# One core, attention times a gated MLP in float32: work queued by the time of its input, sums shared by load, x through two queues, and the first chunk normalised and transposed tile by tile

## The chip, the cores and the metric

The kernel runs on one core of a Trainium2 chip. The number that counts is the device time of one execution in microseconds. Three timed runs of the kernel before lie between 2642.64 and 2644.13 us, with a median of 2642.66 us.

A core has five engines with a queue each: TensorE (PE, matmuls), VectorE (DVE), ScalarE (ACT), GpSimd (POOL) and SyncE (SP), which here does nothing but issue transfers. Each works through its queue in the order in which the program was written; an instruction whose input is missing holds up all that stand behind it on that engine.

## What is computed

With x of 2048 tokens by 576 features, 32 heads of 18 features, and an inner width of 4608:

```python
xn = _layernorm(x, axis=-1)
s = _A_ref(xn, A_wqkv, A_wo)             # softmax attention with 32 heads, then @ wo
g = _silu(_B_ref(xn, B_w_gate, B_w_up, B_w_down))   # ((xn @ w_gate) * (xn @ w_up)) @ w_down
return x + s * g
```

All of it is in float32. Most products are made of two parts: a value is split in a rounded one (the "high" part, written by ACT as float32r) and what is left (the "low" part, a subtraction on DVE or POOL), and the matmul adds high by high, high by low and low by high.

## The kernel before

The program has three stages.

**Opening.** x comes in four chunks of 512 tokens, each of four tiles of 128. `norm_stats` (L287 to L289) and `norm_apply` (L297 to L300) normalise a tile on DVE, with one square root on ACT; `to_columns` (L319 to L327) turns a chunk into columns: PE transposes into PSUM banks, ACT writes the high part, DVE the low one. `qk_block` (L336 to L346) makes 128 of the 1152 columns of q and k for a chunk with 14 matmuls, in the order of the list `PAIRS`; ACT and DVE split the result into one of three `hl` buffers, and SP stores it in DRAM (`sqk`). `w_fetch` loads two blocks of weights, `w_now` splits them (L119 on ACT, L121 on POOL). `v_fetch` loads half of v's weights into a single buffer, which `v_split` (L384, L385) has to have read before the next load. All of this stands in the order of the code.

**Main stage.** `order` writes it with a planner. The array is used as two halves of 64 rows, half 0 and half 1, each with a clock of its own in the plan (`clk`). For each of the 32 heads there are 64 score blocks whose row maxima DVE takes (L541, L543), and 64 blocks made again the other way round, on which ACT takes the exponential (L580, L582); `pv_group` (L591) multiplies them with v on the whole array, three groups a head. Between these the planner spreads the MLP: 72 units, four chunks of tokens (`c`) by 18 steps (`q`). In a unit half 0 makes two "up" blocks and half 1 two "gate" blocks (L629, 27 matmuls each); ACT copies up (`us`, L636), DVE multiplies it with gate (L643), ACT writes the high part `hs` (L646) and POOL the low part (L653). Then both halves make the down products (L677), eight sums a unit. A sum is added to the accumulator by DVE (L734), or copied out by ACT (`st`, L728, two buffers) and added by POOL (L697): the first half of the columns always on DVE, the second always through ACT and POOL (`by_act`).

The planner holds for each engine the time at which it comes free (`free`) and writes an instruction at once when the matmul that it belongs to is written: L646 right after L643, on whose result it waits. Only POOL's work is kept in a list until its input counts as done (`pool_later`). Transfers are written when the planner reaches them, whether or not what they read is made.

**Change of chunk.** While the last gate and up blocks of a chunk run, the tile `xg` that they read is overwritten with the next chunk: after every third matmul one block of x for that half (`x_block`, L356 and L359), ten transfers for each half, all on SP. This happens three times.

**Ending.** The attention's output is multiplied with wo tile by tile (L1249) and joined with g and x.

## Time and profile before

| | us |
|---|---|
| median of the timed runs | 2642.66 |
| the profiled execution: its own time | 2645.09 |
| the profiled execution: span from first to last instruction | 2643.3 |
| PE, DVE, ACT, POOL busy | 2608.3, 1803.8, 1545.8, 663.2 |
| opening: first matmul of `qk_block`, first score block | 16.86, 204.4 |
| main stage, to the first transpose of the ending | 2568.7 |

A page of the profile gives busy time by engine, the chain of work that ended last and the costliest groups of instructions; the trace behind it answers with timelines, with tables of who waited for whom, and with busy time by stretch. PE is busy nearly all the time; a matmul's end is modelled, so PE can count as busy while its next matmul is late.

### The profile page before, as it was taken

How to read it: one execution, taken by the hardware profiler on the slowest of the kernel's cores; microseconds unless marked ns; L12 is line 12 of the kernel's file. 1: busy time of each engine (PE TensorE's matmuls, PEld its weight loads, DVE VectorE, ACT ScalarE, POOL GpSimd, SP SyncE). 2: the span in 40 equal slices, each digit the busy share in tenths (PEclk: the TensorE clock that was granted, in tenths of full speed). 3: DMA queues.
4: the chain of work that ended last, by engine and by line, in shares of the span. 5: the costliest groups of instructions: out<-in, count | busy, mean ns of one | idle time of the engine just before them, and what ended most of it. 6: DMA issues, size and time to landing. Idle time of an engine off the chain costs nothing.

```text
span 2643.3 us, 59231 instructions
## 1 busy us (share of the span) xinstructions
PE 2608.3 (99%) x24504; PEld 2131.3 (81%) x24504; DVE 1803.8 (68%) x3007; ACT 1545.8 (58%) x3096; POOL 663.2 (25%) x683
## 2 busy tenths in 40 slices
PE   7999999999999999999999999999999999999999
PEld 6899888777778887777778877878878778878779
DVE  7218677777777777766667777777767777766336
ACT  4223666666766666656656665666656666656642
POOL 3114543433422112212111211111111212111125
PEclk9999999999999999999999999999999999999999
DMA  6799766676664444464464444444464444533356
GB/s 216 224 302 261 213 192 181 186 189 176 176 172 131 136 145 146 153 168 147 137 171 125 156 142 136 140 127 152 138 161 127 145 135 152 146 123 127 118 195 205
DMA packets 201581, 434.30 MB, mean 164 GB/s; under 512 B 81216, under 2 KB 130784, under 8 KB 167776
## 3 DMA queue, kind: packets, MB, share of 16 engines
q1 hardware_dynamic: 199072, 422.26, 53.8%
q0 software_dynamic: 2240, 8.26, 0.8%
q8 instruction: 192, 3.15, 0.5%
q14 instruction: 77, 0.63, 0.1%
HBM read 314.64 MB, written 110.56 MB: 161 GB/s over the span
## 4 chain that ended last, share of the span: by engine, by line
PE 94%; DMA 2%; DVE 2%; ACT 2%; POOL 0%; issue 0%; SPq 0%; POOLq 0%; ACTq 0%
PE pg L629 34%; PE pg L591 17%; PE pg L677 15%; PE pa L541 10%; PE pb L580 9%; PE pg L1249 2%; PE pg L393 2%; PE pa L336 2%; PE pb L336 2%; ACT pt L582 1%; DMA wor<-in_A_wo_dram 0%; DVE xn L298 0%; DMA xc<-sx 0%; DMA ks<-sqk 0%; DMA swo<-wor 0%; DVE st L287 0%
## 5 line engine op out<-in xcount | busy, mean ns | idle before, releaser
L543 DVE TENSOR_REDUCE mx<-pa 128x1 f32<-128x512 f32 x2016 | 1347.0, 686 | 308.8 <-PE pa L541 175.0
L629 PE MATMUL pg<-xc,wgu 64*128 64x512 f32 x7776 | 1414.2, 393 | 3.7 <-DMA xc<-sx 2.2
L582 ACT ACTIVATE pt<-pb 128x512 f32<-128x512 f32 x2003 | 1135.3, 600 | 462.8 <-PE pb L580 340.9
L629 PEld LDWEIGHTS pg<-xc,wgu 64*128 64x128 f32 x7776 | 1064.2, 186 | 61.4 <-DMA xc<-sx 3.1
L677 PE MATMUL pg<-wd,hs 64*128 64x288 f32 x6816 | 840.2, 293 | 0.0
L677 PEld LDWEIGHTS pg<-wd,hs 64*128 64x128 f32 x6816 | 782.5, 185 | 13.3 <-issue 2.5
L541 PE MATMUL pa<-ks,qs 54*128 54x512 f32 x2016 | 790.8, 400 | 0.2 <-DVE mx L543 0.2
L580 PE MATMUL pb<-qs,ks 56*128 56x512 f32 x2003 | 786.7, 400 | 4.1 <-ACT pt L582 4.1
L591 PE MATMUL pg<-pt,vt 128*32 128x512 f32 x4096 | 459.4, 595 | 4.0 <-ACT st L728 2.3
L653 POOL TENSOR_TENSOR hs<-us,hs 128x512 fp32r<-128x512 f32 x144 | 185.8, 1290 | 1034.1 <-ACT hs L646 940.1
L541 PEld LDWEIGHTS pa<-ks,qs 54*128 54x128 f32 x2016 | 366.7, 185 | 78.3 <-issue 62.2
L580 PEld LDWEIGHTS pb<-qs,ks 56*128 56x128 f32 x2003 | 364.3, 185 | 15.1 <-ACT pt L582 7.4
L697 POOL TENSOR_TENSOR acc<-acc,st 128x288 f32<-128x288 f32 x268 | 216.2, 809 | 563.1 <-ACT st L728 348.0
L591 PEld LDWEIGHTS pg<-pt,vt 128*32 128x32 f32 x4096 | 123.5, 110 | 280.6 <-issue 266.6
L597 DVE TENSOR_TENSOR oc<-oc,pg 128x512 f32<-128x512 f32 x64 | 44.0, 687 | 306.4 <-PE pg L591 306.4
L646 ACT ACTIVATE hs<-us 128x512 fp32r<-128x512 f32 x144 | 91.3, 634 | 115.4 <-DVE us L643 115.3
L208 POOL TENSOR_TENSOR wgu<-wraw,wgu 128x384 fp32r<-128x384 f32 x108 | 108.4, 1014 | 144.3 <-ACT wgu L207 119.5
L734 DVE TENSOR_TENSOR acc<-acc,pg 128x288 f32<-128x288 f32 x277 | 123.1, 445 | 25.2 <-PE pg L677 23.0
L728 ACT ACTIVATE st<-pg 128x288 f32<-128x288 f32 x268 | 111.2, 415 | 27.2 <-PE pg L677 13.3
L643 DVE TENSOR_TENSOR us<-pg,us 128x512 f32<-128x512 f32 x144 | 98.4, 683 | 39.1 <-ACT pt L582 15.0
L636 ACT ACTIVATE us<-pg 128x512 f32<-128x512 f32 x144 | 86.4, 600 | 44.7 <-PE pg L629 38.1
L595 ACT ACTIVATE oc<-pg 128x512 f32<-128x512 f32 x32 | 19.2, 599 | 131.8 <-PE pg L591 131.8
(111 smaller groups left out, 1254.8 us busy)
## 6 DMA issues: line engine op xcount, KB each, us to landing
wgu<-swg SPq DMA_DIRECT2D x102, 1152.0 KB
wd<-swd SPq DMA_DIRECT2D x50, 1152.0 KB
swg<-wgu SPq DMA_DIRECT2D x36, 1152.0 KB
qs<-sqk SPq DMA_DIRECT2D x192, 144.0 KB
ks<-sqk SPq DMA_DIRECT2D x192, 144.0 KB
swd<-wd SPq DMA_DIRECT2D x18, 1152.0 KB
sqk<-hl SPq DMA_DIRECT2D x32, 512.0 KB
xc<-sx SPq DMA_DIRECT2D x48, 256.0 KB
```

The lines of the kernel that those rows point to most:

```text
L208: nc.gpsimd.tensor_tensor(w[:, 9 + b:12 + b, :], raw[:, b:b + 3, :], w[:, b:b + 3, :].bitcast(FT), op=OP.subtract)
L541: nc.tensor.matmul(p, q[rows, t * 128:(t + 1) * 128], k[rows, c * 512:(c + 1) * 512], start=True, stop=True)
L543: nc.vector.tensor_reduce(mx[h][:, t, c:c + 1], p, axis=AX.X, op=OP.max)
L580: nc.tensor.matmul(p, k[rows, t * 128:(t + 1) * 128], q[rows, c * 512:(c + 1) * 512], start=True, stop=True)
L582: nc.scalar.activation(pt[t, c // 2][:, c % 2, :], p, AF.Exp, scale=scale)
L591: nc.tensor.matmul(p[32 * c:32 * c + 32, :], vt[h // 2][:, t, 6 * (h % 2):6 * (h % 2) + 32], pt[t, c // 2][:, c % 2, :], start=t == ts[0], ...
L629: nc.tensor.matmul(ps, gw[n][half[r], a, :], xg[i][half[r], e, :], start=k == 0, stop=k == len(TERMS) - 1)
L653: nc.gpsimd.tensor_tensor(hj[:, 1, :], h32, hj[:, 0, :].bitcast(FT), op=OP.subtract)
L677: op = nc.tensor.matmul(ps[:, 0:HALF], hs[u][half[r], j, a, s * 128:(s + 1) * 128], dw[u][half[r], j, e, i * HALF:(i + 1) * HALF], start=( ...
L697: nc.gpsimd.tensor_tensor(a, a, st, op=OP.add)
L728: nc.scalar.activation(st, ps[:, 0:HALF], AF.Copy)
L734: nc.vector.tensor_tensor(a, a, ps[:, 0:HALF], op=OP.add)
```

## The change

It has five parts.

1. The first chunk is made tile by tile (`first_columns`): a tile is normalised, turned and written before the next one's turn. ACT makes the copy of the last 64 columns that DVE made. POOL's first low part of the weights is held until DVE has normalised the last tile (`behind`, for chunks 0 and 1).
2. `w_now(1)` stands ahead of `norm(1)`; the fifth bank of `to_columns` comes from the q and k banks; `v_fetch(1)` moves from behind block 3 to behind block 5 of chunk 0; `PAIRS` takes the low parts of x ahead of those of the weights.
3. In the main stage ACT's and DVE's work that is fed by another engine is kept in the list `soon` until the planner counts its input as done, and transfers in the list `moves`.
4. A sum goes to ACT and POOL only if a buffer counts as free and ACT is free before DVE.
5. Half 1's blocks of x are issued by POOL, half 0's by SP as before.

```diff
-PAIRS = ([(i, i) for i in range(4)] + [(4 + i, i) for i in range(4)]
-         + [(i, 4 + i) for i in range(4)] + [(8, 8), (9, 8)])
+PAIRS = ([(i, i) for i in range(4)] + [(i, 4 + i) for i in range(4)]
+         + [(8, 8)] + [(4 + i, i) for i in range(4)] + [(9, 8)])
...
+            if behind:
+                after(op, behind.pop(), "DVE's fast mode and Pool share a port")
...
+    def soon_now(now):
+
+        for item in list(soon):
+            at, eng, length, work = item
+            if at <= max(now + 0.1, free[eng]):
+                soon.remove(item)
+                work(engine(eng, at, length))
...
+    def move(at, work):
+        if ordering:
+            moves.append((at, work))
+        else:
+            work()
...
         def end():
             gdone.add(n)
             split_at["g", n] = free["POOL"] + 0.2
-            nc.sync.dma_start(swg[f], w.bitcast(FT))
-            g_load(n + 2)
+
+            def keep():
+                nc.sync.dma_start(swg[f], w.bitcast(FT))
+                g_load(n + 2)
+
+            move(free["POOL"], keep)
...
+        op = nc.vector.tensor_scalar(xn[:, t, 0:D], xin[c][:, t, :], mv[:, 0:1], rs[:, 1:2],
+                                     op0=OP.subtract, op1=OP.mult)
+        if c < 2 and t == 3:
+            behind.append(op)
+        if c:
+            nc.vector.tensor_copy(xn[:, t, D:640], xn[:, t, 512:D])
+        else:
+            nc.scalar.activation(xn[:, t, D:640], xn[:, t, 512:D], AF.Copy)
...
         for k in range(5):
-            p = bank("g", 3)
+            if k < 4:
+                p = bank("g", 3)
+            else:
+                p = bank("a" if nqk[0] % 2 else "b", 2)
+                nqk[0] += 1
...
+    def first_columns():
+
+        xc = xcs[0] = pp.tile([128, 9, 512], FR, name="xcx", bufs=2)
+        ps, last = {}, bank("a", 2)
+
+        def turn(t):
+            ps[t] = bank("g", 3).rearrange("p (k s) -> p k s", k=4)
+            for k in range(4):
+                nc.tensor.transpose(ps[t][:, k, :], xns[0][:, t, k * 128:(k + 1) * 128], ident)
+            nc.tensor.transpose(last[:, t * 128:(t + 1) * 128], xns[0][:, t, 512:640], ident)
+            nc.scalar.activation(xc[:, 0:4, t * 128:(t + 1) * 128], ps[t], AF.Copy)
+
+        def lows(t):
+            cs = slice(t * 128, (t + 1) * 128)
+            nc.vector.tensor_tensor(xc[:, 4:8, cs], ps[t], xc[:, 0:4, cs].bitcast(FT), op=OP.subtract)
+
+        norm_stats(0, 0)
+        norm_stats(0, 1)
+        norm_apply(0, 0)
+        norm_stats(0, 2)
+        turn(0)
+        wq[0], todo = w_split(raws[0], 2)
+        for f, a in todo[:2]:
+            f(*a, rest=False)
+        norm_apply(0, 1)
+        norm_stats(0, 3)
+        turn(1)
+        norm_apply(0, 2)
+        lows(0)
+        norm_apply(0, 3)
+        for f, a in todo[:2]:
+            f(*a, high=False)
+        turn(2)
+        lows(1)
+        turn(3)
+        nc.scalar.activation(xc[:, 8, :], last, AF.Copy)
+        for f, a in todo[2:]:
+            f(*a)
+        lows(2)
+        lows(3)
+        nc.vector.tensor_tensor(xc[64:128, 8, :], last[64:128, :], xc[64:128, 8, :].bitcast(FT), op=OP.subtract)
+        xns.pop(0)
...
+        queue = nc.gpsimd if r else nc.sync
...
-    norm(0)
-    w_now(0)
-    to_columns(0)
+    first_columns()
+    w_now(1)
     norm(1)
-    w_now(1)
...
-                if c == 0:
-                    v_fetch(1)
+            if c == 0 and b == 5:
+                v_fetch(1)
...
+            def high(end):
+                nc.scalar.activation(hj[:, 0, :], h32, AF.Copy)
+                lows.append((n, hj, h32))
+                pool_later.append((end + 0.1, 1.30, low_now))
+                if stacks:
+                    load_stack(*stacks.pop(0))
+                    moved(end + 1.4, 0.88)
...
-        def by_act(u, i):
-            return i == 1 and u < len(units) - 1
+        st_end = []
+
+        def by_act(u, i, at):
+
+            if units[u][1] == 0:
+                return i == 1
+            if u == len(units) - 1 or len(sums_later) == 2 or len(st_end) > 1 and st_end[-2 + len(sums_later)] > at:
+                return False
+            return max(free["ACT"], at) < max(free["DVE"], at)
...
-                            x_block(c + 1, k // 3, (64 * r,))
-                            there["x", c + 1, k // 3, r] = moved(clk[r] + 0.5, 0.262)
+                            x_block(c + 1, k // 3, 64 * r)
+                            if r:
+                                there["x", c + 1, k // 3, r] = engine("POOL", clk[r] + 0.5, 0.75 + 0.6 * (k == 14)) + 3.0
+                            else:
+                                there["x", c + 1, k // 3, r] = moved(clk[r] + 0.5, 0.285)
...
-                if not r and n > 0 and gated.get(n - 1, 1e9) + 2.0 > now:
+                if not r and n > 0 and low_end.get(n - 1, 1e9) > now + 0.4:
...
-                            fin = engine("ACT", done + 0.08, 0.632)
                             loaded[n] = moved(done - 0.4, 1.18) if (n // 2 + 1) % NF2 else 0.0
-                            pool_later.append((fin + 0.1, 1.30, low_now))
-                            if stacks:
-                                load_stack(*stacks.pop(0))
-                                moved(fin + 1.4, 0.88)
+                            soon.append((done + 0.08, "ACT", 0.632, highs[-1]))
```

Four rows of lists show what this makes of the order. First ACT in the opening; `rs` is the square root of a tile of chunk 1, `wgu` the split of the weights (`wraw_111` is the second pair of blocks), `xcx` the columns, `hl` the result of a block. Before:

```order
L326 ACTIVATE xcx_168<-pg_197 128x512
L289 ACTIVATE rs_206<-mv_205,eps_83 128x1
L289 ACTIVATE rs_213<-mv_212,eps_83 128x1
L289 ACTIVATE rs_220<-mv_219,eps_83 128x1
L289 ACTIVATE rs_227<-mv_226,eps_83 128x1
L119 ACTIVATE wgu_245<-wraw_111 128x512
L119 ACTIVATE wgu_245<-wraw_111 128x128
L119 ACTIVATE wgu_245<-wraw_111 128x512
L119 ACTIVATE wgu_245<-wraw_111 128x128
L339 ACTIVATE hl_285<-pb_270 128x512
```

After:

```order
L402 ACTIVATE xcx_118<-pg_189 128x4x128
L427 ACTIVATE xcx_118<-pa_119 128x512
L127 ACTIVATE wgu_152<-wraw_99 128x512
L127 ACTIVATE wgu_152<-wraw_99 128x128
L127 ACTIVATE wgu_204<-wraw_111 128x512
L127 ACTIVATE wgu_204<-wraw_111 128x128
L127 ACTIVATE wgu_204<-wraw_111 128x512
L127 ACTIVATE wgu_204<-wraw_111 128x128
L340 ACTIVATE rs_215<-mv_214,eps_83 128x1
L340 ACTIVATE rs_222<-mv_221,eps_83 128x1
```

The four splits of the second pair stood behind chunk 1's four square roots, which wait for DVE, and stand ahead of them now.

SP in the opening, where `sqk` is the store of a block and `wvraw` the load of v's second half, which waits for POOL to have read the first. Before:

```order
L346 DMA sqk_71<-hl_333 128x2x512
L346 DMA sqk_71<-hl_388 128x2x512
L372 DMA wvraw_430<-in_A_wqkv_dram 128x4x288
L375 DMA wvraw_430<-in_A_wqkv_dram 64x288 x2
L346 DMA sqk_71<-hl_449 128x2x512
L346 DMA sqk_71<-hl_488 128x2x512
L278 DMA xin_492<-in_A_x_dram 128x576 x4
L346 DMA sqk_71<-hl_512 128x2x512
```

After:

```order
L451 DMA sqk_71<-hl_333 128x2x512
L451 DMA sqk_71<-hl_388 128x2x512
L451 DMA sqk_71<-hl_445 128x2x512
L451 DMA sqk_71<-hl_484 128x2x512
L477 DMA wvraw_488<-in_A_wqkv_dram 128x4x288
L480 DMA wvraw_488<-in_A_wqkv_dram 64x288 x2
L329 DMA xin_492<-in_A_x_dram 128x576 x4
L451 DMA sqk_71<-hl_512 128x2x512
```

The load of v's weights moved behind the stores of blocks 4 and 5 of chunk 0.

ACT in the main stage, in the fourth unit; `pt` is an exponential, `us` the copy of up, `hs` the high part of the product, `wgu` and `wd` splits of weights. Before:

```order
L239 ACTIVATE wd_2933<-draw_2523 128x576 x2
L636 ACTIVATE us_2978<-pg_2842 128x512
L582 ACTIVATE pt_2876<-pb_2983 128x512
L582 ACTIVATE pt_2990<-pb_2991 128x512
L646 ACTIVATE hs_2996<-us_2978 128x512
L207 ACTIVATE wgu_2998<-wraw_2648 128x384 x3
L582 ACTIVATE pt_2990<-pb_3069 128x512
L582 ACTIVATE pt_3077<-pb_3078 128x512
```

After:

```order
L286 ACTIVATE wd_2910<-draw_2558 128x576 x2
L754 ACTIVATE us_2978<-pg_2888 128x512
L697 ACTIVATE pt_2856<-pb_2980 128x512
L697 ACTIVATE pt_2985<-pb_2986 128x512
L248 ACTIVATE wgu_2997<-wraw_2655 128x384
L766 ACTIVATE hs_2995<-us_2978 128x512
L248 ACTIVATE wgu_2997<-wraw_2655 128x384 x2
L697 ACTIVATE pt_2985<-pb_3072 128x512
```

One piece of a split has come between the exponentials and `hs`, which waits for DVE's product.

The third change of chunk: SP before, and POOL after (`xc_1446` and `xc_1596` are the two parts of the x tile, `wd` and `wgu` loads of weights, `hs` the low part, `acc` a sum). SP before:

```order
L359 DMA xc_1446<-sx_72 64x1024 x4
L356 DMA xc_1446<-sx_72 64x512
L356 DMA xc_1596<-sx_72 64x512
L359 DMA xc_1446<-sx_72 64x1024
L359 DMA xc_1596<-sx_72 64x1024
L359 DMA xc_1446<-sx_72 64x1024
L359 DMA xc_1596<-sx_72 64x1024
L356 DMA xc_1446<-sx_72 64x512
L356 DMA xc_1596<-sx_72 64x512
L359 DMA xc_1596<-sx_72 64x1024 x6
L233 DMA wd_29092<-swd_74 128x2304
L199 DMA wgu_29108<-swg_73 128x2304
```

POOL after:

```order
L826 TENSOR_TENSOR acc_2345<-acc_2345,st_28317 128x288
L464 DMA xc_1446<-sx_72 64x1024 x2
L779 TENSOR_TENSOR hs_28444<-us_28413,hs_28444 128x512
L464 DMA xc_1446<-sx_72 64x1024 x2
L461 DMA xc_1446<-sx_72 64x512
L461 DMA xc_1596<-sx_72 64x512
L464 DMA xc_1596<-sx_72 64x1024 x4
L826 TENSOR_TENSOR acc_2345<-acc_2345,st_28662 128x288
L779 TENSOR_TENSOR hs_28444<-us_28596,hs_28444 128x512
```

Half 1's ten transfers left SP's list and stand on POOL between the low parts of the last two blocks and the sums.

144 lines of the change are left out of this document (86 added, 58 removed).

## Prediction

> **What bounds the kernel.** I read the page, then busy time by stretch, the waits of PE's two queues, and the timeline of the opening.
>
> ```profile
> span 2643.3 us, 59231 instructions
> ...
> PE 94%; DMA 2%; DVE 2%; ACT 2%; POOL 0%; issue 0%; SPq 0%; POOLq 0%; ACTq 0%
> ```
>
> The second row is the chain that ended last: 94% PE. Stretches give each engine's busy time (PE, its weight loads, DVE, ACT, POOL), the granted clock, the DMA engines' share and GB/s:
>
> ```profile
> 0.00:60.00 60.00, 43.54 (x205) 35.27 (x206) 42.91 (x99) 24.54 (x55) 17.24 (x25) 1.00 0.71 215
> 60.00:205.00 145.00, 144.67 (x833) 129.22 (x831) 29.19 (x57) 39.54 (x87) 22.92 (x24) 1.00 0.84 262
> 205.00:2568.00 2363.00, 2350.84 (x22938) 1898.16 (x22939) 1683.53 (x2767) 1464.83 (x2904) 582.78 (x582) 1.00 0.53 155
> 1150.00:1162.00 12.00, 9.49 (x58) 7.51 (x57) 4.86 (x10) 4.73 (x10) 2.32 (x3) 0.72 0.37 138
> ```
>
> PE is idle for 16.5 us of the first 60, for 0.3 from there to 205, and for 12.2 in the main stage. The last row holds a dip of the granted clock (0.72) with 2.5 us of that idle time. The profiled execution took 2645.09 us, 2.43 more than the timed median; the dip is about that much, and nothing in the change acts on it. The matmuls stay the same in number and shape, so only idle time and late issue can be won.
>
> **The opening, part by part.** The timeline (start, length, engine, line, idle time before it):
>
> ```profile
> 3.65 0.82 DVE L287 BATCH_NORM_STATS2 st<-xin 128x6 f32<-128x288 f32 x2 [2.31 <-DMA xin<-in_A_x_dram]
> ...
> 7.88 0.11 DVE L297 RECIPROCAL rs<-rs 128x1 f32<-128x1 f32 x1
> 8.02 0.58 DVE L298 TENSOR_SCALAR xn<-xin,mv,rs 128x576 f32<-128x576 f32 x1
> ...
> 8.63 0.20 DVE L300 COPY xn<-xn 128x64 f32<-128x64 f32 x1
> ...
> 8.89 3.75 POOL L121 TENSOR_TENSOR wgu<-wraw,wgu 128x512 fp32r<-128x512 f32 x4 [7.81 <-ACT wgu L119]
> 8.94 1.54 DVE L298 TENSOR_SCALAR xn<-xin,mv,rs 128x576 f32<-128x576 f32 x1
> ...
> 14.57 0.69 DVE L323 TENSOR_TENSOR xcx<-pg,xcx 128x512 fp32r<-128x512 f32 x1 [0.97 <-ACT xcx L322]
> ...
> 16.50 0.60 ACT L322 ACTIVATE xcx<-pg 128x512 fp32r<-128x512 f32 x1 [0.26 <-PE pg L319]
> ...
> 16.86 3.46 PE L336 MATMUL pb<-xcx,wgu 128*128 128x512 f32 x14
> ...
> 24.75 2.56 PE L336 MATMUL pb<-xcx,wgu 128*128 128x512 f32 x10 [0.18 <-POOL wgu L121]
> ...
> 27.16 0.49 PE L319 MATMUL pg<-ident,xn 128*128 128x128 f32 x3
> ...
> 28.82 1.64 PE L319 MATMUL pg<-ident,xn 128*128 128x128 f32 x13 [1.18 <-DVE xn L298]
> ...
> 31.70 0.66 PE L319 MATMUL pg<-ident,xn 128*128 128x128 f32 x4 [1.24 <-DVE xcx L323]
> ...
> 32.12 3.45 PE L336 MATMUL pa<-xcx,wgu 128*128 128x512 f32 x14
> ...
> 51.19 0.60 ACT L339 ACTIVATE hl<-pa 128x512 fp32r<-128x512 f32 x1 [5.20 <-DMA sqk<-hl]
> 51.49 1.91 PE L319 MATMUL pg<-ident,xn 128*128 128x128 f32 x16
> ...
> 55.67 3.47 PE L336 MATMUL pa<-xcx,wgu 128*128 128x512 f32 x14
> ```
>
> *The first chunk.* The statistics of four tiles take from 3.65 to 7.88. The first scaling takes 0.58 us, the next 1.54: POOL has begun its split at 8.89. The change holds POOL back until the fourth scaling, gives the copies of 0.20 to ACT, and lets PE and ACT turn early tiles while DVE does late ones. By these rows the fourth tile is scaled after 4.2 us of statistics, four times 0.8 (0.11 and 0.58 with the gaps between) and one low part of 0.69 written ahead of it: 3.65 + 4.2 + 3.2 + 0.7 = 11.8. Behind it lie ACT's copy (0.20) and two high parts (0.60 each), so the first block starts at about 13.2, for 16.86: 3.7 us. The low parts of tiles 2 and 3 end at about 14, when the block gets to them after four matmuls of some 0.23; so the changed order of products costs nothing. The weights' low parts, now from 11.8, are needed after nine, at 15.3; two pieces last 2 us (four took 3.75).
>
> The Trainium skill (SBUF — State Buffer, Who interferes with whom) says that DVE's scaling in its fast mode and a POOL instruction lock each other out of a shared port for a whole instruction. The rows 0.58 and 1.54 agree; by that rule alone, three held scalings give back three times 0.96, 2.9 of the 3.7.
>
> *Chunk 1's columns.* Before, the transposes start at 27.16, wait for a scaling and then for a bank, and the next block starts at 32.12. Twenty at the pace of 16 in 1.91 take 2.4, so 2.6 are lost; some 0.5 more go ahead of 24.75, because the second weights' split stood behind chunk 1's square roots. Both causes go: the split stands ahead, and the fifth bank doesn't wait for DVE. What is late next is chunk 1's fourth scaling. DVE is done with chunk 0 at about 14.5; statistics of 4.2, one scaling of 1.54 beside POOL's second split, three of 0.8 and three copies of 0.2 put it at 23.3, against a third block that ends at 13.2 + 3 x 3.3 = 23.1. I leave 0.6 for it: 2.5.
>
> *Chunk 2's columns.* From 51.49 to 55.67 where 2.4 are needed: 1.8 lost, because ACT had waited 5.20 us for a store that stood on SP behind the load of v's weights. That load moves behind two more stores; `v_split` reads it behind block 3 of chunk 1, four blocks of 3.3 us on, which hides it.
>
> The opening's sum is 3.7 + 2.5 + 1.8 = 8.0, between 3.7 (the first block alone) and 9.5 (nothing late anywhere). PE's 0.3 idle us from 60 to 205 show that nothing waits there, so the gain reaches the main stage; the DMA engines' 0.84 leaves them 23 us.
>
> **The main stage.** What ended the waits (us in total, times, longest):
>
> ```profile
> PEld pb L580 <- ACT pt L582: 7.4, 12, 2.9
> PEld pg L591 <- ACT st L728: 4.9, 9, 1.7
> PEld pg L591 <- DVE acc L734: 3.8, 11, 0.7
> PEld pg L629 <- DMA xc<-sx: 3.1, 2, 2.0
> ...
> PEld pg L591 <- DVE mx L543: 2.4, 8, 0.4
> ...
> PEld pg L629 <- ACT st L728: 1.6, 3, 1.0
> PEld pa L541 <- DVE mx L543: 1.4, 5, 0.5
> PEld pg L591 <- ACT pt L582: 1.3, 6, 0.3
> PEld pg L629 <- ACT us L636: 1.0, 1, 1.0
> ```
>
> On ACT's own queue the same table, and the two kinds of sums and the add behind them as groups (instructions, busy us, mean ns, idle time before):
>
> ```profile
> ACT hs L646 <- DVE us L643: 115.3, 139, 2.0
> ...
> ACT st L728 <- POOL acc L697: 10.6, 10, 1.4
> ```
>
> ```profile
> L697 POOL TENSOR_TENSOR acc<-acc,st 128x288 f32<-128x288 f32 x268 | 216.2, 809 | 563.1 <-ACT st L728 348.0 <-PE pg L677 77.1 <-PE pa L541 52.6
> ...
> L734 DVE TENSOR_TENSOR acc<-acc,pg 128x288 f32<-128x288 f32 x277 | 123.1, 445 | 25.2 <-PE pg L677 23.0 <-PE pa L580 1.5
> L728 ACT ACTIVATE st<-pg 128x288 f32<-128x288 f32 x268 | 111.2, 415 | 27.2 <-PE pg L677 13.3 <-POOL acc L697 10.6 <-PE pb L580 0.6
> ```
>
> The weight loads waited 26.9 us by these rows for ACT (16.2), DVE (7.6) and x (3.1), and 30 with the smaller ones: more than PE's idle 12.2, because a matmul's modelled end covers part of it. The longest, 2.9, lies in the dip; without it ACT's share is 13.3 and all of it 27.
>
> *ACT's queue.* `hs` stood there 0.83 us (115.3 by 139) before its input came, and `st` 1.1 us for a buffer; exponentials behind them came late, which is the first row. Now other work fills both gaps. I take half of ACT's 13.3, as an exponential is late too when ACT is simply full: 6.5.
>
> *Sums by load.* In the changed order ACT and POOL take 293 of the sums where they took 268, DVE 252 for 277: 25 times 0.45 us less on DVE, as many of 0.42 more on ACT and of 0.81 on POOL, which is busy for 583 of the stage's 2363 us. It counts as nothing.
>
> ```profile
> L770 POOL DMA_DIRECT2D sg<-sil x12 | 7.1, 591 | 3.6 <-POOL sil L763 3.3 <-PE pg L677 0.3
> ...
> POOL hs L653 <- ACT hs L646: 940.1, 121, 14.9
> ...
> 1969.73 8.35 DMA xc<-sx
> ```
>
> *x by two queues.* The last row, from the chain, is the one change of chunk that was late. Thirty issues move to POOL, at 0.59 us as for `sg`: 5.9 us a change, plus waiting for PE's last read of each piece. Behind them on POOL stand the last block's low part and the sums; up's next copy and the down products wait for that low part. Half of x's 3.1 is won: 1.5. Transfers queued later take waiting off SP and nothing off PE: nothing.
>
> So the main stage gives 8, between 27 (all of it) and a loss: a new order can make waits of its own, bounded by the 7.6 that DVE's rows show unforeseen.
>
> **Sum.** 2645.1 - 8.0 - 8.0 = 2629.1 for an execution with the dip, less 2.43 for the median: **2627 us**.
>
> **Rivals.**
> - *The waits only change place.* The plan's errors stay, and other work is late instead: only the opening is won, 2642.7 - 8 = 2635. For it: DVE's rows, which the change hardly touches; against it: `st`, which waited for a known cause.
> - *Nearly all waits go.* Opening 9.5, main stage 27: 2642.7 - 36.5 = 2606. Against it: DVE has nearly as much to do as before.
> - *No change to speak of.* Opening 3.7, main stage as much worse: 2643.
> - *POOL holds the change of chunk (slower).* POOL waits for PE's reads in order, the low part comes late, ACT's copy of up waits for it, and the exponentials behind that. If each change costs the 8.4 us of the chain's row above, 25 in all: 2642.7 - 16 + 25 = 2652. It decides from 5.3 us a change on, a third of the 16 won elsewhere. Against it: POOL waited for ACT 940.1 us in all before low parts, so there is room.
> - *DVE starves POOL's issues (slower).* If DVE holds up each of the thirty issues by the 0.96 us of the scaling's pair and all of it reaches PE, 29 us: 2656. Against it: 12 issues at 0.59 amid DVE's work.
>
> The Trainium skill (SBUF — State Buffer, SBUF: two separate sides) has this as a rule: GpSimd cannot write its transfers' descriptors while DVE runs a fast-mode instruction. The `sg` row shows no such wait.
>
> **How the numbers follow.** Forecast 0.52 (2619 to 2633 for itself), waits change place 0.17, nearly all go 0.15, no change 0.08, POOL holds the change 0.05, starving 0.03. The first three hold 0.84 and reach from 2606 to 2635, and with an opening of 3.7 to 2640: range 2606 to 2640. A difference of 0.2%, 5.3 us, is about what a measurement tells from no change: faster 0.84, same 0.08, slower 0.08.
>
> **What would show it.** The first block at 13 to 13.5; no gap over 1 us among chunk 1's and 2's transposes; the first score block at about 196; scalings of chunk 0 all near 0.58. In the main stage `hs` waiting less than 60 us for DVE and `st` not for POOL; the weight loads' waits near 18; POOL's x issues near 0.6 each, and no wait of PE for x. The prediction is wrong if PE waits at the changes of chunk for low parts, if DVE's reduces end more waits than before, or if stores hold the opening again.

## The result, and the profile after

The changed kernel takes 2620.65 us (median of four runs, 2617.51 to 2621.97) against 2642.65 for the kernel before: 22.0 us less, a ratio of 0.9914 with an interval of 0.9897 to 0.9931. 2627 was predicted, in a range of 2606 to 2640; the forecast's own range began at 2619.

The profiled execution took 2617.51 us, the shortest of the four. The span and the chain that ended last, on its page:

```profile
span 2615.7 us, 59267 instructions
...
PE 98%; DMA 1%; DVE 1%; ACT 0%; issue 0%; SPq 0%; POOL 0%; POOLq 0%; ACTq 0%
```

Busy time by stretch, with the columns of the prediction's table:

```profile
0.00:60.00 60.00, 52.78 (x245) 43.33 (x246) 43.35 (x111) 27.60 (x67) 19.77 (x30) 1.00 0.76 237
60.00:196.00 136.00, 136.00 (x789) 122.35 (x787) 22.93 (x40) 36.09 (x77) 19.62 (x21) 1.00 0.85 266
196.00:2539.00 2343.00, 2340.00 (x22947) 1892.56 (x22946) 1684.34 (x2744) 1488.66 (x2930) 616.44 (x637) 1.00 0.53 157
2539.00:2615.70 76.70, 68.85 (x528) 68.00 (x527) 47.19 (x84) 16.83 (x52) 40.27 (x52) 0.97 0.64 219
1150.00:1162.00 12.00, 12.00 (x110) 9.45 (x110) 7.69 (x14) 6.83 (x14) 2.09 (x2) 1.00 0.62 221
```

PE idles 7.2 us of the first 60 where it was 16.5, none up to the main stage, and 3.0 in the main stage where it was 12.2. In the last row PE is busy throughout at a full granted clock; at that place the kernel before ran at 0.72. By stage, the first score block comes at 196.14 instead of 204.4, 8.25 us earlier; the main stage is 21.6 us shorter between the two profiled executions, and the ending 2.2 longer. Those executions lie 27.6 us apart and the medians 22.0, so by the medians the main stage is worth about 22.0 - 8.25 + 2.2 = 16 us.

The opening of the changed kernel, from the timeline of DVE and of PE:

```profile
5.62 0.58 DVE L349 TENSOR_SCALAR xn<-xin,mv,rs 128x576 f32<-128x576 f32 x1
...
10.28 0.58 DVE L349 TENSOR_SCALAR xn<-xin,mv,rs 128x576 f32<-128x576 f32 x1
...
20.98 0.58 DVE L349 TENSOR_SCALAR xn<-xin,mv,rs 128x576 f32<-128x576 f32 x1
...
12.71 5.46 PE L441 MATMUL pb<-xcx,wgu 128*128 128x512 f32 x14 [0.47 <-ACT xcx L402]
18.01 3.34 PE L441 MATMUL pa<-xcx,wgu 128*128 128x512 f32 x14
21.19 3.34 PE L441 MATMUL pb<-xcx,wgu 128*128 128x512 f32 x14
24.37 1.91 PE L381 MATMUL pg<-ident,xn 128*128 128x128 f32 x16
26.11 0.60 PE L381 MATMUL pa<-ident,xn 128*128 128x128 f32 x4
26.47 3.47 PE L441 MATMUL pb<-xcx,wgu 128*128 128x512 f32 x14
...
45.86 1.91 PE L381 MATMUL pg<-ident,xn 128*128 128x128 f32 x16
47.60 0.60 PE L381 MATMUL pb<-ident,xn 128*128 128x128 f32 x4
47.96 3.44 PE L441 MATMUL pa<-xcx,wgu 128*128 128x512 f32 x14
```

The transposes of chunks 1 and 2 now run without a gap, and every scaling of chunks 0 and 1 takes about 0.6 us. One row is new: the first block starts 4.15 us earlier than before but lasts 5.3 us to the next one's start, where its neighbours last 3.2.

What the weight loads of the main stage waited for, the rows that answer to those of before:

```profile
PEld pg L706 <- ACT st L856: 2.5, 9, 0.8
PEld pg L706 <- ACT pt L697: 2.1, 7, 0.4
PEld pg L706 <- DVE mx L646: 2.1, 8, 0.4
PEld pa L644 <- DVE mx L646: 1.6, 4, 0.6
...
PEld pg L706 <- DVE acc L862: 1.2, 3, 0.7
...
PEld pg L748 <- DMA xc<-sx: 0.7, 1, 0.7
PEld pb L695 <- ACT pt L697: 0.6, 3, 0.2
...
PEld pg L799 <- ACT us L754: 0.2, 1, 0.2
```

They sum to 11.0 us where the prediction's nine rows had 26.9: ACT 5.4 for 16.2 (2.9 of which lay in the dip), DVE 4.9 for 7.6, x 0.7 for 3.1. On ACT's own queue, `hs` waits 12.0 us for DVE instead of 115.3, and `st` no longer waits for POOL:

```profile
ACT hs L766 <- DVE us L761: 12.0, 7, 8.2
```

The groups of the sums and of POOL's issues:

```profile
L826 POOL TENSOR_TENSOR acc<-acc,st 128x288 f32<-128x288 f32 x293 | 236.0, 810 | 498.2 <-ACT st L856 255.5 <-PE pg L799 118.4 <-PE pa L644 58.4
L856 ACT ACTIVATE st<-pg 128x288 f32<-128x288 f32 x293 | 120.6, 412 | 25.8 <-PE pg L799 18.7 <-PE pb L695 2.1 <-PE pa L644 0.8
L464 POOL DMA_DIRECT2D xc<-sx x24 | 12.6, 525 | 37.1 <-PE pg L748 18.7 <-PE pa L644 9.8 <-PE pg L799 6.7
```

### The profile page after: what moved, and what is told of

Same layout as the page of the kernel before. It is cut to its first block, busy times and chain, and to the rows that moved or that the text cites. A ratio compares the mean times of both kernels' runs of the same rounds, so it can differ in the third digit from the quotient of the medians.

```text
span 2615.7 us, 59267 instructions
## 1 busy us (share of the span) xinstructions
PE 2597.6 (99%) x24504; PEld 2126.2 (81%) x24504; DVE 1797.8 (69%) x2978; ACT 1569.2 (60%) x3125; POOL 696.1 (27%) x738
## 4 chain that ended last, share of the span: by engine, by line
PE 98%; DMA 1%; DVE 1%; ACT 0%; issue 0%; SPq 0%; POOL 0%; POOLq 0%; ACTq 0%
PE pg L748 35%; PE pg L706 17%; PE pg L799 16%; PE pa L644 11%; PE pb L695 8%; PE pb L441 2%; PE pg L1380 2%; PE pg L498 2%; PE pa L441 2%; DMA xc<-sx 1%; DMA oin<-so 0%; PE pa L695 0%; PE pb L1357 0%; DVE mx L646 0%; PE pg L381 0%; DMA xin<-in_A_x_dram 0%
## 5 line engine op out<-in xcount | busy, mean ns | idle before, releaser
L697 ACT ACTIVATE pt<-pb 128x512 f32<-128x512 f32 x2003 | 1153.9, 601 | 515.5 <-PE pb L695 381.9
L748 PE MATMUL pg<-xc,wgu 64*128 64x512 f32 x7776 | 1389.9, 392 | 0.6 <-DMA xc<-sx 0.5
L748 PEld LDWEIGHTS pg<-xc,wgu 64*128 64x128 f32 x7776 | 1053.2, 186 | 55.2 <-issue 1.7
L799 PE MATMUL pg<-wd,hs 64*128 64x288 f32 x6816 | 823.8, 293 | 0.0
L799 PEld LDWEIGHTS pg<-wd,hs 64*128 64x128 f32 x6816 | 773.2, 185 | 12.6 <-issue 2.5
L826 POOL TENSOR_TENSOR acc<-acc,st 128x288 f32<-128x288 f32 x293 | 236.0, 810 | 498.2 <-ACT st L856 255.5
L856 ACT ACTIVATE st<-pg 128x288 f32<-128x288 f32 x293 | 120.6, 412 | 25.8 <-PE pg L799 18.7
L862 DVE TENSOR_TENSOR acc<-acc,pg 128x288 f32<-128x288 f32 x252 | 112.7, 448 | 32.5 <-PE pg L799 30.1
L766 ACT ACTIVATE hs<-us 128x512 fp32r<-128x512 f32 x144 | 90.6, 629 | 12.2 <-DVE us L761 12.0
```

Of the source, the lines that this page charges most:

```text
L697: nc.scalar.activation(pt[t, c // 2][:, c % 2, :], p, AF.Exp, scale=scale)
L748: nc.tensor.matmul(ps, gw[n][half[r], a, :], xg[i][half[r], e, :], start=k == 0, stop=k == len(TERMS) - 1)
L799: op = nc.tensor.matmul(ps[:, 0:HALF], hs[u][half[r], j, a, s * 128:(s + 1) * 128], dw[u][half[r], j, e, i * HALF:(i + 1) * HALF], start=( ...
L826: nc.gpsimd.tensor_tensor(a, a, st, op=OP.add)
L856: nc.scalar.activation(st, ps[:, 0:HALF], AF.Copy)
L862: nc.vector.tensor_tensor(a, a, ps[:, 0:HALF], op=OP.add)
```

## The experiments

A reckoning is used throughout: the **lost time** of the main stage is its length, from the first score block to the first transpose of the ending, less what its matmuls take when they follow one another without a gap. Those prices are from dense stretches of the traces: 0.233 us for 512 columns on half the array and 0.134 for 288, two such matmuls running side by side, and 0.107 for one of the value product. It includes waits that a matmul's modelled end hides. A **change of chunk** is counted from 2 us before the first issue of x to 16 us after the last. "Half clock" lists stretches in which the trace's record of the granted clock says 0.5.

| | time | lost | at the three changes of chunk | elsewhere | half clock, main stage |
|---|---|---|---|---|---|
| before | 2642.65 | 77.7 | 5.9 | 71.8 | 6.8 |
| opening alone (e1) | 2634.65 | 72.9 | 5.8 | 67.1 | none |
| before, other order (e2) | 2657.33 | 89.2 | 9.1 | 80.0 | 3.4 |
| before, pause (e11) | 2654.47 | 91.9 | 9.5 | 82.4 | 6.8, 3.4, 3.4 |
| changed | 2620.65 | 56.1 | 2.7 | 53.4 | none |
| changed, other order (e3) | 2634.30 | 71.4 | 16.7 | 54.7 | 6.8, 6.8 |
| fed work at once (e4) | 2655.24 | 94.3 | 24.4 | 69.9 | 3.4, 3.4, 6.8 |
| all x on SP (e5) | 2616.56 | 57.1 | 3.7 | 53.4 | none |
| fixed sums (e6) | 2636.66 | 77.3 | 16.5 | 60.8 | 3.4, 6.8 |
| transfers at once, POOL free (e7) | 2624.28 | 60.5 | 6.7 | 53.8 | none |
| warm opening (e8) | 2619.27 | 58.0 | 4.1 | 53.9 | none |
| e3's order, all x on SP (e9) | 2624.94 | 65.2 | 12.4 | 52.8 | 10.2 |
| same setting, x counted later (e10) | 2630.45 | 70.4 | 10.6 | 59.8 | 6.8 |
| best (e12) | 2614.79 | 56.4 | 2.6 | 53.8 | none |

The times are medians; lost time and clock are of one profiled execution each. In e3 and e10 the half clock behind the second change reaches past its window, so that 1 to 2 us of it stand under "elsewhere".

**The opening alone.** The kernel before with parts 1 and 2 of the change (`first_columns`, the order of `w_now` and `norm`, the fifth bank, `v_fetch`, `PAIRS`), and its main stage as it was.

```diff
-    norm(0)
-    w_now(0)
-    to_columns(0)
-    norm(1)
+    first_columns()
     w_now(1)
+    norm(1)
```

> The kernel before with the change's opening alone (parts 1 and 2); the planner and all of the main stage's order stay as before. Theory A (the opening's gain arrives whole, 8.3 us by the two traces: the first score block at 204.4 before and 196.1 after; the rest is the main stage): about 2634.5 us, the first score block near 196, and the main stage as long as before. Rival B (the opening's gain is eaten later by transfers, and the main stage has won all 22): 2640 to 2643.

Measured: 2634.65 us, 0.9968 of the kernel before (0.9955 to 0.998), 9.0 less than the 2643.69 of the runs beside it; the first score block at 196.2. So the opening is worth 8 to 9 us, and the rest of the 22 comes from the main stage.

**Another order, nothing else.** One number of the planner (`TAIL`) goes from 40 to 41, once in the kernel before, once in the changed one.

```diff
-        EASE, TAIL, PACE, SKEW, PULL, FIRST = 1.0, 40, 1.005, 1.0, 3.0, 0.4
+        EASE, TAIL, PACE, SKEW, PULL, FIRST = 1.0, 41, 1.005, 1.0, 3.0, 0.4
```

> The kernel before with one constant of the planner's pace changed, TAIL from 40 to 41, which writes the same work in another order and changes no rule. Theory A (the new rules win the main stage's 14 us): within 3 us of 2642.7. Rival C (any new order moves the time by many us, and the main stage's gain is luck of the order): 5 us or more away, on either side.

> The changed kernel with the same constant changed, TAIL from 40 to 41. Theory A: within 3 us of 2620.7. Rival C: 5 us or more away, on either side; then no single undone part of the main stage can be told from luck below that size.

Measured: 2657.33 (1.0054, 1.004 to 1.0068) and 2634.30 (0.9966, 0.9954 to 0.9979), each some 14 us above its own kernel. A whole kernel's time thus says little about one rule of the planner, since any rule also redraws the order; the verdicts below go by stage. Even away from the changes of chunk the redrawn order moved the lost time, by 8.2 us in the kernel before (71.8 to 80.0) and by 1.3 in the changed one: differences below that size need a second sign, such as the kind of wait. In e3 the loss lies at the changes of chunk (16.7 us), elsewhere it is the changed kernel's (54.7 against 53.4). PE waits of e3, 740 to 790 us:

```profile
PE pg L748 <- DMA xc<-sx: 6.9, 3, 5.5
```

After the longest of these waits PE ran 6.8 us at half clock.

**Fed work at once.** The changed kernel, but the row maxima's two small pieces and `hs` are written when the planner meets them, not when their input counts as done.

```diff
-                            soon.append((done + 0.08, "ACT", 0.632, highs[-1]))
+                            highs[-1](engine("ACT", done + 0.08, 0.632))
...
-            soon.append((at + 0.08, "ACT", 0.25, high))
+            high(engine("ACT", at + 0.08, 0.25))
...
-                soon.append((end + 0.08, "DVE", 0.15, low))
+                low(engine("DVE", end + 0.08, 0.15))
```

> The changed kernel with ACT's and DVE's fed work (the high part hs, the two parts of the negated maxima) written at once again instead of when its input counts as done. Theory A (half of ACT's waits were due to it, 6.5 us): 2627, and ACT waits over 100 us for DVE before hs, near 60 or less in the changed kernel. Rival C: the wait comes back, and the time is within 3 us of 2620.7.

Measured: 2655.24 (1.0045, 1.0032 to 1.0057), 34.6 above the changed kernel. ACT's queue in the main stage:

```profile
ACT hs L766 <- DVE us L761: 111.4, 136, 1.9
```

and what PE itself waited for:

```profile
PE pg L748 <- DMA xc<-sx: 4.8, 3, 2.6
PE pg L799 <- POOLq L803: 4.7, 2, 2.9
PE pg L748 <- ACT us L754: 2.6, 2, 1.4
```

`hs` stands in ACT's queue as it did before, and 16.5 us more are lost away from the changes of chunk (69.9 against 53.4), twice what a redrawn order did to the kernel before. But the path that the prediction had for it doesn't show. The weight loads, up to 2540 us:

```profile
PEld pg L706 <- DVE acc L862: 4.9, 12, 0.8
...
PEld pg L706 <- ACT pt L697: 1.1, 3, 0.4
```

The exponentials (`pt`), which the prediction held to be late behind `hs`, hold them up for 1.1 us, less than in the changed kernel (2.7); the waits for DVE's sums grew (from 1.2). Away from the changes all such waits rose by 5.4 us only, from 12.9 to 18.3, so most of the 16.5 lies in no wait that the trace names. The rest is lost at the changes. There POOL, the engine that in this kernel issues half of x, holds others up: L803 is a mark on POOL's queue that hands a bank to half 1.

**All x on SP.** The changed kernel with both halves' x issued by SP, and with the planner's account of them as before; TensorE's order in the main stage stays the same.

```diff
-        queue = nc.gpsimd if r else nc.sync
+        queue = nc.sync
...
-                            if r:
-                                there["x", c + 1, k // 3, r] = engine("POOL", clk[r] + 0.5, 0.75 + 0.6 * (k == 14)) + 3.0
-                            else:
-                                there["x", c + 1, k // 3, r] = moved(clk[r] + 0.5, 0.285)
+                            there["x", c + 1, k // 3, r] = moved(clk[r] + 0.5, 0.262)
```

> The changed kernel with both halves' x on SP's queue, as in the kernel before; everything else, and the order of TensorE's main stage, is the changed kernel's. In what follows, lost time is the elapsed time of the main stage less what its matmuls take one after the other by their own durations; by that reckoning the kernel before loses 77.7 us, the changed one 56.1, and of these 2.7 in the three changes of chunk. Theory (splitting x over two queues is worth nothing much, since POOL's transfers land only after 6 to 14 us and the readers come late enough): the changes of chunk lose 3 to 9 us, elsewhere 53 to 55, 2618 to 2624 us in all. Rival (as the prediction had it, one queue per half lets x be there in time, 1.5 us per run): 2619 to 2623 too, but with TensorE waiting in the changes of chunk for x issued by SP. Second rival (one queue is too slow for the denser order): over 10 us lost in the changes, one or more stretches at half clock there, 2630 or more.

Measured: 2616.56 (2615.84 to 2618.14; 0.9898, 0.9885 to 0.9912). The changes of chunk lose 3.7 us instead of 2.7. Part 5 of the change therefore wins 1 us at most in this order. The kernel without it is 4.1 us faster by the medians, but the two intervals overlap, and of the two profiled executions it is the one without part 5 that is longer, by 0.6 us of span; so a gain of either isn't shown. Seen beside it on PE's timeline, with the same instructions in the opening as in the changed kernel:

```profile
11.73 0.27 PE L401 MATMUL pa<-ident,xn 128*128 128x128 f32 x1
12.58 3.47 PE L441 MATMUL pb<-xcx,wgu 128*128 128x512 f32 x14 [0.58 <-ACT xcx L402]
15.88 3.34 PE L441 MATMUL pa<-xcx,wgu 128*128 128x512 f32 x14
```

Here the first block lasts 3.3 us, not 5.3. Yet the first score block comes at 196.5, no earlier than in the changed kernel, because the first value products now wait for the split of the second half of v's weights:

```profile
60.10 0.40 PE L498 MATMUL pg<-wv,xcx 128*128 128x288 f32 x1 [0.30 <-POOL wv L490]
```

They last 17.3 us, from 55.65 to 72.99, where they took 14.85 in the changed kernel (from 57.77) and in the kernel before. In e4, where the first block was fast too, the first score block came at 197.3.

**Fixed sums.** The changed kernel with the old rule for the sums, and with the wait for a free `st` buffer that went with it.

```diff
-            if units[u][1] == 0:
-                return i == 1
-            if u == len(units) - 1 or len(sums_later) == 2 or len(st_end) > 1 and st_end[-2 + len(sums_later)] > at:
-                return False
-            return max(free["ACT"], at) < max(free["DVE"], at)
+            return i == 1 and u < len(units) - 1
...
+                    while len(sums_later) == 2:
+                        pool_now()
```

> The changed kernel with the sums of the value product going to ACT or DVE by the old fixed rule (ACT for the second, DVE for the first and for the last unit) instead of by which engine is free sooner. Theory of the prediction (sums by load are worth 0): 53 to 56 us lost away from the changes of chunk, as in the changed kernel; the total is 2621 plus what the order happens to cost at the changes of chunk (0 to 14 us). Rival (sums by load carry a third of the main stage's gain): 58 to 62 us lost away from the changes of chunk, and more waits of TensorE for the engine that the rule fixes.

Measured: 2636.66 (0.9972, 0.996 to 0.9983). Away from the changes 60.8 us are lost against 53.4, and `st` waits for POOL again:

```profile
ACT st L854 <- POOL acc L822: 6.0, 7, 1.4
...
PEld pg L706 <- ACT st L854: 4.8, 8, 1.7
```

With the 2.3 us of gate and up's weight loads, TensorE's weight loads wait 7.1 us for `st`, as much as in the kernel before (7.1), where the changed kernel has 2.5. So the rival holds: the fixed rule makes TensorE wait for the engine that it names. The size is less certain: 7.4 us by the lost time, 4.6 by these waits, and a redrawn order alone has moved the lost time by as much (e2). The other 13.8 us are lost at the changes, as in e3.

**Transfers at once; POOL not held.** Two parts undone that lie in different stages.

```diff
-        if ordering:
-            moves.append((at, work))
-        else:
-            work()
+        work()
...
-        if c < 2 and t == 3:
-            behind.append(op)
```

> The changed kernel with two parts undone that lie in different stages, so that each is read by its stage: transfers behind a finished piece are written at once again (main stage), and POOL's splits of weights no longer wait for DVE's scaling (opening). Theory: the late transfers are worth 0 (prediction): 53 to 56 us lost away from the changes of chunk. POOL's wait is worth 1 us or so of the opening: one or more scalings of chunk 0 take 1.5 us instead of 0.58, the first block of the opening starts 13.5 to 14.5 instead of 12.71, the first score block at 196.5 to 197.5. Rivals: late transfers carry a third of the gain: 58 us or more away from the changes; the wait is worth nothing because the slow scalings hide behind the loading of the tiles: first block still at 12.7.

Measured: 2624.28 (0.9926, 0.9914 to 0.9939). Away from the changes 53.8 us are lost, as in the changed kernel: the late transfers are worth nothing there. At the changes 6.7 are lost for 2.7, and PE waits 2.5 us for x instead of 0.5; e8, whose main stage is the changed kernel's, loses 4.1, so up to 4 us of the late transfers' worth may lie there. In the opening, from the timelines of DVE and PE:

```profile
8.81 1.34 DVE L346 TENSOR_SCALAR xn<-xin,mv,rs 128x576 f32<-128x576 f32 x1
...
23.52 2.21 DVE L346 TENSOR_SCALAR xn<-xin,mv,rs 128x576 f32<-128x576 f32 x1
...
13.29 4.90 PE L436 MATMUL pb<-xcx,wgu 128*128 128x512 f32 x14 [0.47 <-ACT xcx L397]
...
25.79 1.64 PE L376 MATMUL pg<-ident,xn 128*128 128x128 f32 x13 [0.92 <-DVE xn L346]
```

The first score block comes at 198.4, 2.3 us later. The first block starts 0.6 late, but the second one starts at 18.03, as in the changed kernel (18.01). What stays lost is 1.1 us in chunk 1's transposes, which its last scaling, 2.21 us long, holds up (3.24 us to the next block for 2.10), and 1.1 in the first value products, which wait for POOL's split of v's weights (15.9 us for 14.85). So holding POOL matters for the second chunk, not for the first. The Trainium skill (SBUF — State Buffer, Who interferes with whom) lets one of the two engines block until the other's whole instruction is over; 1.34 and 2.21 us, against 0.58 where POOL is held, agree.

**A warm opening.** 37 transposes of the identity matrix, which nobody reads, are added: 22 ahead of chunk 0's and a few behind each of its turns.

```diff
+        idle = bank("b", 2)
+
+        def warm(n):
+            for _ in range(n):
+                nc.tensor.transpose(idle[:, 0:128], ident, ident)
...
+        warm(22)
```

> The changed kernel with 37 added transposes of the identity matrix into a bank that is free in the opening: 22 ahead of the first transposes of chunk 0, and 5, 4, 2 and 4 behind its four turns; their results are read by nobody. It asks why the first block of the opening takes 5.3 us in the changed kernel (12.71 to 18.01; its first matmuls come 0.428 us apart, then 0.233) and 3.3 in the kernel before, where 20 transposes ran right ahead of it. Theory (TensorE runs slower after a stretch in which it had little to do, whatever the granted clock in the records says, and the sparse transposes of the tile-by-tile opening don't bring it up): first block in 3.3 to 3.5 us from 12.7 to 12.9, first score block at 194.0 to 194.6 instead of 196.14, in all 2 us less: 2618 to 2619.5. Rival (the first matmuls wait for something else, such as the low parts of x or the split of the weights, and the spacing of 0.428 is theirs): the block still takes 5 us or more, nothing gained, 2620 to 2622.

Measured: 2619.27 (0.9909, 0.9896 to 0.9923). PE's timeline:

```profile
1.39 4.96 PE L401 MATMUL pb<-ident 128*128 128x128 f32 x22 [1.39 <-DVE ident L101]
...
12.24 3.53 PE L452 MATMUL pb<-xcx,wgu 128*128 128x512 f32 x14
15.60 3.33 PE L452 MATMUL pa<-xcx,wgu 128*128 128x512 f32 x14
...
60.10 0.40 PE L509 MATMUL pg<-wv,xcx 128*128 128x288 f32 x1 [0.29 <-POOL wv L501]
```

The block takes 3.4 us and the second one starts 2.4 us earlier than in the changed kernel: dense transposes ahead of it do bring the block to its full pace. But the first score block still comes at 196.5, where 194.0 to 194.6 was expected, and the time can't be told from the changed kernel's, as the intervals overlap. The lead was given back at 55 to 73 us, where the first value products met the split of the second half of v's weights.

**Why e3 loses at the changes of chunk.** Two kernels take e3's setting (41). In the first, only the queue of half 1's x changes, SP for POOL, and TensorE, DVE and ACT do the same instructions in the same order. In the second the planner counts x as there 10 us later on POOL and 8 later on SP.

```diff
-        queue = nc.gpsimd if r else nc.sync
+        queue = nc.sync
```

```diff
-                                there["x", c + 1, k // 3, r] = engine("POOL", clk[r] + 0.5, 0.75 + 0.6 * (k == 14)) + 3.0
+                                there["x", c + 1, k // 3, r] = engine("POOL", clk[r] + 0.5, 0.75 + 0.6 * (k == 14)) + 13.0
...
-                                there["x", c + 1, k // 3, r] = moved(clk[r] + 0.5, 0.285)
+                                there["x", c + 1, k // 3, r] = moved(clk[r] + 0.5, 0.285) + 8.0
```

> The order of e3_order_after, in which the three changes of chunk lost 10.2, 5.6 and 0.9 us and TensorE fell to half clock in two of them, with x of the second half issued from SP instead of POOL; nothing else is moved, TensorE, DVE and ACT do the same instructions in the same order. Theory (the transfers issued by POOL land late, 14 to 18 us after they are issued, and that is what the changes of chunk paid for): the three changes lose 2 to 6 us together instead of 16.7, no stretch at half clock there, 2620 to 2626 us instead of 2634.3. Rival (that order asks for x too early whichever queue brings it): 10 us or more lost in the changes, 2630 to 2636.

> Again the number of e3_order_after (41), POOL still issuing x, but the planner counts x as there 10 us later on POOL's queue (13.0 behind the issue instead of 3.0) and 8 later on SP's, so that it puts the first readers of x later in the order. Theory (the planner places the readers by a landing time that is too short): the changes of chunk lose 1 to 4 us and none at half clock, 2620 to 2626. Rival (readers put off leave TensorE short of other work at the changes): waits for other inputs take the place, 8 us or more lost there, 2630 or more.

Measured: 2624.94 (0.9934, 0.9919 to 0.9948) and 2630.45 (0.9954, 0.9939 to 0.9969). Neither theory holds whole. With SP the second change of chunk loses 0.6 us instead of 5.6, but the first 10.9, as before; PE there, 740 to 790 us:

```profile
PE pg L748 <- DMA xc<-sx: 7.0, 1, 7.0
```

With x counted later the first change loses 2.2 us instead of 10.2, but the second 7.6, again for x; PE at 1335 to 1372 us:

```profile
PE pg L748 <- DMA xc<-sx: 4.3, 2, 3.5
```

In e3 transfers issued by POOL landed up to 18.4 us after their issue where the planner counts 3.0; that goes with the loss of the second change, which SP's queue takes away. The loss of the first change isn't POOL's: in e3 the longest wait there ended with a block that SP had issued 13.2 us before (750.15 to 763.38, by the chain), and with SP alone the loss is as large. There this order asks for x before either queue can bring it. In both kernels PE waits for x, and nothing else, in the change of chunk that costs most.

**A pause behind a load.** In the kernel before, the planner hands out no small work for 16 us, not 6, after the load of a part of wo.

```diff
-                        quiet[0] = now + (16.0 if name == "last" else 6.0)
+                        quiet[0] = now + (16.0 if name in ("last", "fetch") else 6.0)
```

> The kernel before with one number of the change: the planner hands out no other small work for 16 us, instead of 6, after it has issued the load of a part of the output weights (wor), so that ACT's rounding of that part is not written ahead of the load's end. In the kernel before ACT stood 7.1 us in all for these loads, 3.4 of it at 1149.3 to 1152.8; TensorE waited 2.5 us there and then ran 6.8 us at half clock. Theory: ACT waits under 1 us for these loads, the 13 us from 1149 on lose under 1 us instead of 5.7, and no half clock there; in all 2637 to 2640 plus what the changed order behind that place costs (up to 14 either way, by e2_order_before). Rival (the half clock comes at that place by itself, without the wait): it is still there, and the time stays 2642 to 2644.

Measured: 2654.47 (1.0044, 1.0027 to 1.0061). The stretch in which the kernel before waited and fell to a lower clock:

```profile
1149.00:1162.00 13.00, 13.00 (x147) 12.97 (x145) 11.39 (x20) 10.12 (x20) 5.32 (x6) 1.00 0.75 193
```

ACT no longer waits for these loads at all (7.1 us before), and the stretch is full at a full clock: this line, which is part of the changed kernel, takes the stall away in this order. It isn't the only thing that can: in e2, which doesn't have it, ACT waits for none of these loads either, and the clock stays full at that place. The time nevertheless rose by 12 us, because the order behind that place is another one, with stalls of its own. So what the line is worth in the changed kernel can't be read from this run's total.

**The best.** The changed kernel with all x on SP, the added transposes, and the second half of v's weights split earlier.

```diff
+        if c == 1:
+            v_split(1)
         for b in range(3, 6):
             qk_block(b, c)
...
-            if c < 2 and b == 3:
-                v_split(c)
+            if c == 0 and b == 3:
+                v_split(0)
```

> The changed kernel with three things on top: both halves' x on SP's queue (e5), the added transposes of the opening (e8), and the split of the second half of the value weights five ACT instructions earlier, ahead of the fourth projection of chunk 1 instead of behind it. In e8 the opening was 2.4 us ahead at 24 and at 55 us, and gave it back at the first value products, which waited for that split (ACT 57.0 to 58.7 and POOL to 61.6, behind a store that held ACT's buffer). Theory: first block in 3.3 us, value products from 55 without waits, first score block at 193.8 to 194.6, 2613.5 to 2616 us. Rival (something further on holds the opening to its time, such as the next weights' load): first score block at 196 or later, 2616 to 2619.

Measured: 2614.79 (2613.56 to 2615.33; 0.9894, 0.9879 to 0.9909), 5.9 us under the changed kernel, whose fastest run (2617.51) is slower than the slowest of these. PE's timeline:

```profile
12.31 3.44 PE L452 MATMUL pb<-xcx,wgu 128*128 128x512 f32 x14
...
55.35 4.94 PE L509 MATMUL pg<-wv,xcx 128*128 128x288 f32 x36
...
193.72 0.50 PE L657 MATMUL pa<-ks,qs 54*128 54x512 f32 x2
```

The lead of 2.4 us now lasts to the first score block, at 193.7.

## Why the prediction was right, and where it was not

**The opening: 8.0 predicted, 8.25 measured.** The mechanism was right in each part. That the sum came out so close is partly luck, since two errors cancel: the first block ran slower than any step had it, and the columns gained more than was priced.

- *The first chunk, 3.7.* The first block started 4.15 us earlier, at 12.71 instead of the predicted 13.2, but it then ran 2.0 us longer, which no step of the prediction had. The prediction priced its matmuls at 0.23 us; after the first, eight came 0.427 apart.
- *Chunk 1's columns, 2.5.* From the first block's start to the next block behind the transposes it was 15.26 us and is now 13.76. With the 2.0 lost in the first block inside, the columns gained 3.5. The scaling counted at 1.54 us beside POOL took 0.62, since the hold acts on chunk 1 as well, and nothing is late there.
- *Chunk 2's columns, 1.8.* 4.18 us are now 2.10: 2.1.

These rows give 7.7. The last half microsecond is chunk 3's columns, which the prediction left out: from the first transpose to the next block it was 2.59 us (89.89 to 92.48) and is 2.10 (82.16 to 84.26).

What the prediction didn't ask is whether the split of v's second half, whose load it held to be hidden, is done in time itself. In the changed kernel it is, because the slow first block left it time enough. Where the first block ran at full pace (e4, e5, e8), the value products waited for that split, and the first score block came at 197.3, 196.5 and 196.5 instead of 196.14. The 2.0 us of the first block therefore cost the opening nothing as long as the split stood where it did; with both mended (e12) it gains 10.7. The most that the prediction allowed, 9.5, was too little for that, and its own rows give only 3.7 + 3.1 + 1.8 = 8.6 for it.

**The main stage: 8 predicted, about 16 measured.** Here the terms were mis-sized.

- *ACT's queue: "I take half of ACT's 13.3": 6.5.* Counted as there, without the 2.9 of the dip, ACT's waits fell from 13.3 to 5.4 us: 7.9. With fed work written at once again, 16.5 us more are lost away from the changes of chunk, so the rule was priced too low. The path isn't borne out: `hs` waits 111.4 us again in e4, and the waits for exponentials, which were to come late behind it, don't return (1.1 us against 2.7). By what path `hs` costs TensorE time stays open. The reason given for half, that an exponential is late too when ACT is simply full, isn't borne out by the mean load: ACT is busy for more of the stage than before (1489 us against 1465). What the remaining 5.4 us are due to wasn't asked.
- *Sums by load: "It counts as nothing".* This step failed: 7.4 us by the lost time of e6, 4.6 by the waits for `st` that it brings back. The waits for `st` and for DVE's sum in the prediction's rows were 10.3 us (4.9, 3.8 and 1.6) and are 3.7. The prediction priced the engines' work, 25 sums of some 0.4 us, and not the matmul that waits for a particular engine to empty its bank. The figures of e4 and e6 overlap, as each was measured with the other rule in place, so they don't add up to a sum.
- *x by two queues: 1.5.* Not there. With all x on SP the changes lose 1 us more, and the whole is no slower. PE waits for x for 0.5 us in the changed kernel and 0.9 with all x on SP, where it was 2.2 before; so it is mostly the order and not the second queue that took these waits away.
- *Transfers queued later: nothing.* Right away from the changes of chunk, by e7; at the changes up to 4 us, which one execution doesn't settle.
- *"the dip is about that much, and nothing in the change acts on it".* The second half of this failed. The changed kernel holds a line that its five parts don't name: it lengthens the pause after a load of wo, and with it alone ACT's wait ahead of the dip is gone (e11). The changed kernel has neither wait nor dip; whether by this line or by its other order isn't shown, since e2 lost both without the line. The kernel before doesn't always dip there: in e1, with the same main stage, PE waited 2.0 us at that place and kept its clock.

In all, the nine rows of weight-load waits fell by 15.9 us of 26.9 (13.0 without the dip's 2.9), and the stage by about 16: a microsecond of wait less was worth a microsecond or a little more. The other kernels of the table bear that out in the rough. Against the changed kernel, their lost time is higher by 0.9 to 2.1 times as much as all waits of weight loads for an engine or a transfer are (13.8 us in the changed kernel, 21.4 in e10, 31.2 in e6, 32.1 in e4), e12 apart, where neither differs by half a microsecond. The prediction's rule of a half was near for ACT's row; what it left out is DVE's rows (7.6, which fell by 2.7) and part of x's.

**The ending** was left at nothing and costs 2.2 us: the first joined tile waits for its stored columns (`oin` from `so`, 1.0 us on PE, 1.2 on the weight load). Which part of the change does it wasn't tried. It isn't the opening, as the ending takes 74.8 us in e1 and 74.7 before; in e9, with the other order and all x on SP, it takes 74.9 for the changed kernel's 76.9.

**The rivals.** "The waits only change place" falls: away from the changes of chunk less is lost in both orders tried (53.4 and 54.7, against 67.1 and 71.8 with the old rules in the order of before and 80.0 in the other). "POOL holds the change of chunk" didn't happen in the changed kernel but did close by: in e4 PE waited 4.7 us for POOL's queue. It was given 0.05. The 6.9 us that PE waited in e3 aren't this rival, as e9 lost as much there with no x on POOL. "DVE starves POOL's issues" falls: 30 issues at 0.52 us. Of the signs, those of the opening came true, but for the first block, which came at 12.71, ahead of the 13 to 13.5; `hs` fell to 12.0 us and `st` no longer waits for POOL; the weight loads' waits went to 11 where 18 was expected; POOL's issues took 0.52 us each, and PE still waited 0.5 us for x where none was expected.

## What to carry to other kernels

Where one engine is nearly always busy, add up what its instructions (its weight loads too) waited for, by releaser, and price every row, those for emptied banks too: here a microsecond of such wait taken away was worth a microsecond or a little more, and six tenths of the sum went. How busy the named engine is on average doesn't tell how much of its row can go. Where a planner writes the order, read an edit by stage and by kind of wait, since an irrelevant number of the planner alone moved this kernel by 14 us. And when an early stage is sped up, look for the next fixed date behind it: the warm opening won 2.4 us that the split of v's weights took back until it was moved as well.
